# Attention block on one core: VectorE's share of the softmax exponentials as a sum of four 16-bit patterns

## The chip, the core and the metric

The kernel runs on one core of a Trainium2 chip. The metric is the device time of one launch in microseconds (us), lower is better. A core has five engines that run their own instruction streams and meet at semaphores: TensorE (PE, matmuls; its weight loads are shown as PEld), VectorE (DVE), ScalarE (ACT), GpSimd (POOL) and SyncE (SP, which issues the DMAs). Matmuls write to PSUM, eight banks of 512 fp32 columns on 128 partitions.

## What is computed

A transformer block on 2048 tokens of width 640: a layer norm, attention with 32 heads of 20 dimensions without a mask, a residual, a second layer norm, and a gated GELU network of width 1728 with a residual.

```python
def _A_ref(x, wqkv, wo):                      # x is layernorm(A_x)
    qkv = (x @ wqkv).reshape(B, S, 3, H, Dh).transpose(2, 0, 3, 1, 4)
    q, k, v = qkv[0], qkv[1], qkv[2]          # B=1, H=32, S=2048, Dh=20
    scores = jnp.einsum("bhqd,bhkd->bhqk", q, k) * (Dh ** -0.5)
    o = jnp.einsum("bhqk,bhkd->bhqd", _softmax(scores), v)
    return o.transpose(0, 2, 1, 3).reshape(B, S, D) @ wo
h  = A_x + _A_ref(_layernorm(A_x), A_wqkv, A_wo)
n  = _layernorm(h)
h2 = h + (gelu(n @ w_gate) * (n @ w_up)) @ w_down
```

The 32 x 2048 x 2048 scores are 134 million exponentials, on 128 partitions about a million columns.

## The kernel before

**Tiling.** Heads go in groups of four (`NG` = 8): head j of a group uses row strip j of the array for its scores (20 dimensions in 32 rows, `tile_position=(32*j, 0)`) and column strip j for its values (21 columns, the last one sums the exponentials), so that four small matmuls run side by side. Queries are cut in chunks of 512, 512, 256, 256, 256, 128 and 128 (`SIZES`, numbered 0 to 6). A *tile* is one PSUM bank of scores, 128 keys by 512 queries or the same number of columns from more key blocks. A *slot* is 64 tiles that accumulate in one output bank: one group of heads in chunks 0 and 1, two in chunks 2 to 4, four in chunks 5 and 6; 32 slots in all. A *quad* is the four tiles of the four heads of a group for the same keys.

**Units.** `units` cuts the tiles of a slot into score units of two or three banks (`PAT`): banks 0 to 2 and 3 to 4 in turn, or, in chunks 1 to 3, banks 0 to 2 and 3 to 5. For each unit, `unit()` issues the score matmuls (L873), one ACT exp over the unit's banks into a ring of bf16 buffers (`pts` with `PR` = 12 tiles and `pts2` with `PR2` = 6), and value matmuls for two quads at a time (`PV_QUADS`) into bank 6. When a slot is complete, `epilogue()` copies bank 6 out, transposes and normalises.

**VectorE's share.** Some tiles per slot (`D_PER_SLOT`: 8 in most, 2 in the first) get their exponential from VectorE, in `d_exp`: the scores are scaled to int16 with 512 steps per octave (L831), and for two tiles at a time six operations correct the mantissa with a quadratic and give the bit pattern of a bf16. In the units of two banks (chunks 0 and 4 to 6) such a tile gets a bank of its own out of the background banks `BG`; in the units of three (chunks 1 to 3) it takes the place of one of ACT's. Its value matmul is put behind the unit at least `D_LAG` = 8 units later.

**Background.** While a chunk's exps run, `post()` does the output projection, the second layer norm and the gated network of the chunk before, in matmuls at low priority (L631, L1061, L1118) with VectorE emptying their banks. After the last chunk this work is the tail of the kernel.

**The order.** The order on each engine comes from a list scheduler (`Sched`) that runs at build time with costs written into each `op`: it walks through planned time, takes the ready operation of best priority (`P_QK` 0 for scores, `P_PV` 1 for values, `P_BG` 3 for background), and holds back a PE operation that would run past the moment at which the next scores are due. The engines then execute that order as it stands, each waiting at its semaphores. The scheduler also keeps the array busy: behind a value operation it adds filler matmuls (`sc.pad`, zeros into bank 6) until a window of 3.4 us is filled to `PAD_MIN`, and in empty moments it issues a full-width one (`sc.warm`). The filler behind value operations hangs on the tag of the operation:

```python
if e == "pe" and self.pad is not None and o.tag and o.tag[0] == "O":
```

Of the kernel before, what the change touches and what calls it, by code (L numbers as in the profile page):

```python
# [7 lines left out]
ALU = mybir.AluOpType  # L8
AX = mybir.AxisListType
FP32 = mybir.dt.float32  # L10
BF16 = mybir.dt.bfloat16
I32 = mybir.dt.int32
F16 = mybir.dt.float16
# [30 lines left out]
class Sched:  # L44
# [46 lines left out]
    def schedule(self):  # L91
# [23 lines left out]
        while done < total:  # L115
# [4 lines left out]
            for e in ENGINES:  # L120
# [8 lines left out]
                while ready[e]:  # L129
# [3 lines left out]
                    if e == "pe" and due is not None and o.prio[0] > 0 and t < due < t + o.dur + (MODE_SWITCH[e] if mode[e] not in (None, o.mode) else 0):  # L133
                        skipped.append((p, i))
                        if len(skipped) >= 60:
                            break
                        continue
# [165 lines left out]
VW = 21  # L303
# [15 lines left out]
CA, CB, CC = -0.277383, 1.25604202, 1.0 - 11.0 / 128  # L319
PV_QUADS = 2  # L320
D_LAG = 8
PR, PR2 = 12, 6
ND = 4
D_PER_SLOT = (8,8,8,8,8,8,6)
D_SLOT0 = 2
D_FIRST, D_SPAN = 1, 16
# [6 lines left out]
def bass_sequential_preLN__mha_block__glu_gated_geglu__prompt_kernel(  # L333
# [12 lines left out]
    with ExitStack() as es:  # L346
# [48 lines left out]
        E_WORDS = 19200  # L395
# [39 lines left out]
        dv = [ka[:, 1024 * i:1024 * i + 1024].bitcast(I16) for i in range(ND - 2)]  # L435
        pts2 = carve(PR2 * 512)


        carve = carver(qt_all[:, 0, :, :].rearrange("p g s -> p (g s)"), NG * 512)
        dv += [carve(1024).bitcast(I16) for _ in range(2)]  # L440
        df1 = carve(1024)
        dw1 = carve(1024).bitcast(F16)
        dv0 = [ha_f[:, 1024 * i:1024 * i + 1024].bitcast(I16) for i in range(ND)]
        df0, dw0 = ha_f[:, 1024 * ND:1024 * ND + 1024], ha_f[:, 1024 * ND + 1024:1024 * ND + 2048].bitcast(F16)
# [336 lines left out]
        PAT = [((0, 1, 2), (3, 4, 5)) if c in (1,2,3) else ((0, 1, 2), (3, 4)) for c in range(len(CHUNKS))]  # L781
        units, ubank, dtile, ends = [], [], [], []
        i, in_slot = 0, {}
        while i < len(tiles):
            s_ = tiles[i][0]
            c = slots[s_][0]
            bs = PAT[c][len(units) % 2]
            k = in_slot.setdefault(s_, [0, 0])
            nd = D_PER_SLOT[c] if s_ else D_SLOT0
            units.append(tiles[i:i + len(bs)])  # L790
            ubank.append(bs[0])
            six = len(PAT[c][1]) == 3
            i += len(units[-1])
            want = min(nd, (k[0] - D_FIRST) * nd // D_SPAN + 1) if k[0] >= D_FIRST else 0
            if six and k[1] < want and len(units[-1]) == 3 and units[-1][2][0] == s_:
                dtile.append(units[-1].pop())
                k[1] += 1
            elif not six and k[1] < want and tiles[i][0] == s_:
                dtile.append(tiles[i])
                k[1] += 1  # L800
                i += 1
            else:
                dtile.append(None)
            k[0] += 1
            ends.append(i)
        assert all(k[1] % 2 == 0 for k in in_slot.values())
        d_tiles = set(x for x in dtile if x)
        x_unit = {}
        for u, tl in enumerate(units):
            for x in tl + [dtile[u]]:  # L810
                x_unit[x] = u
        pv_bank = {}
        pv_open = set()
        pv_wait = []
        last_qk = {c: [] for c in range(len(CHUNKS))}
        d_raw, d_done = [], []
        d_n = [0]
        d_ops = []
# [3 lines left out]
        def d_exp(b, tile, prio):  # L822

            i, h = (d_n[0] // 2) % ND, d_n[0] % 2
            d_n[0] += 1
            assert all(x[1] != ("dv", i) for x in d_done)
            early = slots[tile[0]][0] == 0
            v = (dv0 if early else dv)[i]
            df, dw = (df0, dw0) if early else (df1, dw1)
            aft = tuple(e_ops) if early else tuple(e_ops) + tuple(last_qk[0])  # L830
            d_ops.append(op("dve", lambda eng: eng.tensor_scalar(v[:, 512 * h:512 * h + 512], bank(b), EXP_MUL, -32000.0,  # L831
                                                                 ALU.mult, ALU.max), c_dve(512), P_QK,
                            reads=[("SD", tile)], writes=[("dv", i)], rel=[b], after=aft))
            d_raw.append(tile)
            if h == 0:
                return
            zi = df.bitcast(I16)
            d = lambda fn, n, r, w: d_ops.append(op("dve", fn, 0.066 + n, prio, reads=r, writes=w))
            d(I("tensor_scalar", zi, v, 511, 2048, ALU.bitwise_and, ALU.bitwise_or), 0.265, [("dv", i)], ["df"])
            d(I("tensor_scalar", dw, zi, CA / OCT, CB, ALU.mult, ALU.add), 0.265, ["df"], ["dw"])  # L840
            d(I("tensor_tensor", dw, dw, dw, ALU.mult), 0.53, ["dw"], ["dw"])
            d(I("tensor_tensor", dw, dw, zi, ALU.mult), 0.53, ["df", "dw"], ["dw"])
            d(I("tensor_tensor", v, v, dw, ALU.add), 0.53, ["dw", ("dv", i)], [("dv", i)])
            d(I("tensor_scalar", v, v, 0.25, 16256.0 + 128.0 * (CC - 1.0), ALU.mult, ALU.add), 0.265, [("dv", i)], [("dv", i)])
            for k, tl in enumerate(d_raw):
                d_done.append((v[:, 512 * k:512 * k + 512].bitcast(BF16), ("dv", i), tl))
            d_raw.clear()

        def unit(u):
# [56 lines left out]
            while pv_wait:  # L906

                quads = []
                while pv_wait and len(quads) < PV_QUADS:
                    x0 = pv_wait[0][2]  # L910
                    have = [x for x in pv_wait if x[2][:3] == x0[:3]]
                    want = 4 - sum(1 for j in range(4) if x0[:3] + (j,) in d_tiles)
                    if len(have) < want or quads and quads[0][0][2][0] != x0[0]:
                        break
                    del pv_wait[0:want]
                    quads.append(have)
                if not quads:
                    return
                s_ = quads[0][0][2][0]
                c, gs = slots[s_]  # L920
                q0, nq = CHUNKS[c]
                nk = 512 // nq
                final = quads[-1][0][2][1:3] == (gs[-1], NT // nk - 1)
                if len(quads) < PV_QUADS and not final:
                    pv_wait[0:0] = [x for h in quads for x in h]
                    return

                for have in quads:
                    for x in list(d_done):
                        if u - x_unit[x[2]] >= D_LAG and x[2][3] not in [y[2][3] for y in have]:  # L930
                            have.append(x)
                            d_done.remove(x)
                while final and d_done:
                    have = []
                    for x in list(d_done):
                        if x[2][3] not in [y[2][3] for y in have]:
                            have.append(x)
                            d_done.remove(x)
                    quads.append(have)
                if s_ not in pv_bank:  # L940
                    pv_bank[s_] = bk = Bank(6)
                    acq = [bk]
                else:
                    bk, acq = pv_bank[s_], []
                fns, reads = [], ["vones", "zer"] + k_keys[0][0]
                for have in quads:
                    for kk in range(nk):
                        for pt, pkey, (_, g, kb, j) in have:
                            kt = kb * nk + kk
                            o = 512 * 6 + nq * gs.index(g)  # L950
                            fns.append(I("matmul", PS[32 * j:32 * j + VW, o:o + nq], v_all[:, kt, 4 * g + j, :],
                                         pt[:, kk * nq:(kk + 1) * nq], start=(s_, j) not in pv_open, stop=(kt == NT - 1),
                                         tile_position=(0, 32 * j), skip_group_check=True))
                            pv_open.add((s_, j))
                            reads += [pkey, ("v", kt, g // 4)]
                pv = op("pe", fns, 0.218 * len(quads), P_PV, mode="col", util=0.213 * len(quads), reads=reads, writes=[("O", s_), "pvseq"], acq=acq)
                if final:
                    sc.final.add(pv)
                    assert not d_done and not d_raw
                    epilogue(s_, bk)  # L960

# [182 lines left out]
        for s_, (c, gs) in enumerate(slots):  # L1144
# [27 lines left out]
            while ui < len(units) and ends[ui] - len(units[ui]) < slot_end[s_]:  # L1172
                unit(ui)
                ui += 1
# [36 lines left out]
```

## Time and profile before

| What | us |
|---|---|
| time, median of 3 runs | 927.22 |
| lowest and highest run | 923.36, 928.9 |
| profiled execution, span | 923.6 |
| ACT busy | 887.4 (96%) |
| PE busy | 835.0 (90%) |
| VectorE busy | 760.3 (82%) |
| POOL busy | 34.4 (4%) |
| exps of ACT, all forms (busy) | 954.0 |
| fillers of zeros, L354 `ps<-kt_all,zer` (busy) | 51.9 |
| mean granted TensorE clock | 0.996 |

The span is that of one profiled execution, from the first to the last instruction; it stands at the lower end of the runs. Busy times of one group count each instruction from its start to its end, and instructions of an engine overlap at their ends (that is how the exps' 954.0 fit into 887.4), so the spacing of starts, not the mean duration, tells what one more of a kind costs. A line such as L354 is that of a helper which many operations go through; the names of what is written and read tell them apart.

### The profile page before, as it was taken

To read this page: it belongs to the slowest core of one execution; us is meant where nothing else is said; L and a number is where in the kernel's file an instruction comes from. 1 tells how busy PE (TensorE), PEld (TensorE's weight loads), DVE (VectorE), ACT (ScalarE), POOL (GpSimd) and SP (SyncE) were. 2 spreads that over 40 slices of the span, in tenths; PEclk is the share of its full clock that TensorE was granted. 3 is DMA by queue.
4 is the path that set the end of the run, shared out by engine and by line. 5 is a ranking of instruction groups with operands and counts; after the bars stand their busy time and mean duration, and the time that the engine had idled before them with its cause. 6 is when DMAs were issued, how large, how long until landed. Compare 5 with 4: busy or idle time off the path is not lost.

```text
span 923.6 us, 23026 instructions
## 1 busy us (share of the span) xinstructions
PE 835.0 (90%) x10070; PEld 353.3 (38%) x10070; DVE 760.3 (82%) x1562; ACT 887.4 (96%) x786; POOL 34.4 (4%) x117
## 2 busy tenths in 40 slices
PE   3999999999998997999788997889999999998998
PEld 2432232222222222233233332334445455565666
DVE  8859999899897896888698995878898769997653
ACT  7899999999999999999999999999999999999981
POOL 5000000000001000000001000000101000001000
PEclk9999999999999999999999999999999999999999
DMA  7301021222721000000111000000100000110000
GB/s 258 95 21 41 17 55 48 71 56 67 228 99 30 1 2 1 1 8 16 37 30 30 2 2 1 2 23 24 44 17 16 1 9 23 26 37 10 10 16 16
DMA packets 39516, 34.36 MB, mean 37 GB/s; under 512 B 19436, under 2 KB 36936, under 8 KB 39416
## 3 DMA queue, kind: packets, MB, share of 16 engines
q1 hardware_dynamic: 39416, 32.89, 12.6%
q8 instruction: 79, 1.29, 0.6%
q14 instruction: 21, 0.17, 0.1%
HBM read 20.12 MB, written 8.09 MB: 31 GB/s over the span
## 4 chain that ended last, share of the span: by engine, by line
ACT 73%; PE 20%; DVE 4%; DMA 2%; SPq 0%; issue 0%
ACT pts L354 46%; ACT rege L354 26%; PE ps L873 5%; PE ps L1061 5%; PE ps L354 4%; PE ps L631 3%; PE ps L1118 3%; DMA regw<-in_A_wqkv_dram 1%; DVE rege L354 1%; ACT L354 1%; DVE rege L831 1%; DVE qt_all L354 1%; PE ps L576 0%; DMA rege<-o_nat 0%; DVE rege L1107 0%; SPq L354 0%
## 5 line engine op out<-in xcount | busy, mean ns | idle before, releaser
L354 ACT ACTIVATE pts<-ps 128x1536 bf16<-128x1536 f32 (+1 forms) x474 | 573.2, 1378 | 5.6 <-PE ps L873 4.5
L873 PE MATMUL ps<-qt_all,kt_all 32*128 32x256 bf16 (+2 forms) x3584 | 289.6, 289 | 48.9 <-ACT pts L354 28.3
L354 ACT ACTIVATE rege<-ps 128x1536 bf16<-128x1536 f32 (+1 forms) x230 | 292.1, 1380 | 2.1 <-PE ps L873 1.1
L873 PEld LDWEIGHTS ps<-qt_all,kt_all 32*128 32x128 bf16 x3584 | 91.3, 92 | 271.5 <-ACT pts L354 155.9
L1061 PE MATMUL ps<-rege,regw 128*128 128x256 bf16 (+2 forms) x980 | 159.2, 292 | 10.5 <-DVE rege L1107 4.8
L354 DVE TENSOR_TENSOR qt_all<-qt_all 128x1024 f16<-128x1024 f16 (+1 forms) x235 | 160.6, 683 | 3.3
L831 DVE TENSOR_SCALAR rege<-ps 128x512 int16<-128x512 f32 x152 | 104.3, 686 | 39.7 <-PE ps L873 38.8
L354 PE MATMUL ps<-pts,v_all 128*21 128x256 bf16 (+2 forms) x2122 | 136.3, 290 | 0.0
L354 PE MATMUL ps<-rege,v_all 128*21 128x256 bf16 (+2 forms) x1278 | 108.2, 292 | 0.0
L1061 PEld LDWEIGHTS ps<-rege,regw 128*128 128x128 bf16 x980 | 73.3, 98 | 70.9 <-issue 24.1
L631 PE MATMUL ps<-regw 128*128 128x512 bf16 (+1 forms) x360 | 87.0, 350 | 2.9 <-DVE v_all L764 1.4
L1118 PE MATMUL ps<-regw,rege 128*128 128x320 bf16 x448 | 78.3, 301 | 2.6 <-DVE rege L1107 1.6
L354 DVE TENSOR_SCALAR qt_all<-qt_all 128x1024 int16<-128x1024 int16 (+1 forms) x188 | 75.9, 420 | 1.5
L831 DVE TENSOR_SCALAR qt_all<-ps 128x512 int16<-128x512 f32 x94 | 64.3, 684 | 3.3 <-PE ps L873 3.0
L354 DVE TENSOR_TENSOR rege<-rege 128x1024 f16<-128x1024 f16 (+4 forms) x103 | 65.4, 644 | 0.8
L354 PEld LDWEIGHTS ps<-pts,v_all 128*21 128x21 bf16 x2122 | 49.2, 91 | 38.2 <-issue 32.6
L354 DVE TENSOR_SCALAR rege<-rege 128x1024 int16<-128x1024 int16 (+2 forms) x136 | 55.4, 424 | 1.2
L354 PE MATMUL ps<-kt_all,zer 128*32 128x512 bf16 x608 | 51.9, 385 | 0.0
L1107 DVE TENSOR_TENSOR rege<-rege,ps 128x512 bf16<-128x512 bf16 (+1 forms) x53 | 35.8, 678 | 19.3 <-PE ps L1061 19.1
L1118 PEld LDWEIGHTS ps<-regw,rege 128*128 128x128 bf16 x448 | 36.9, 98 | 32.2 <-issue 12.4
L354 PEld LDWEIGHTS ps<-rege,v_all 128*21 128x21 bf16 x1278 | 39.2, 91 | 19.8 <-issue 14.5
L631 PEld LDWEIGHTS ps<-regw 128*128 128x128 bf16 x360 | 28.6, 98 | 47.1 <-issue 21.9
(95 smaller groups left out, 579.3 us busy)
## 6 DMA issues: line engine op xcount, KB each, us to landing
rege<-in_A_x_dram SPq DMA_DIRECT2D x6, 640.0 KB, 5.3
q_rows<-regw SPq DMA_DIRECT2D x20, 128.0 KB, 1.7
out_dram<-rege SPq DMA_DIRECT2D x16, 160.0 KB, 1.8
regw<-in_B_w_gate_dram SPq DMA_DIRECT2D x1, 2160.0 KB, 11.5
regw<-in_B_w_up_dram SPq DMA_DIRECT2D x1, 2160.0 KB, 16.5
regw<-in_B_w_down_dram SPq DMA_DIRECT2D x1, 2080.0 KB, 21.6
kt_all<-k_rows SPq DMA_DIRECT2D x12, 160.0 KB
qt_all<-q_rows SPq DMA_DIRECT2D x12, 160.0 KB
```

Of the source, the lines that this page charges most:

```text
L354: return lambda eng: getattr(eng, method)(*args, **kwargs)
L631: yield op("pe", lambda eng, l=l, r=r, k=k: eng.matmul(bank(bk, n), l, r, start=(k == 0), stop=(k == len(steps) - 1)), c_mm(n), prio, mode ...
L831: d_ops.append(op("dve", lambda eng: eng.tensor_scalar(v[:, 512 * h:512 * h + 512], bank(b), EXP_MUL, -32000.0, ALU.mult, ALU.max), c_dve( ...
L873: return lambda eng: eng.matmul(out()[:, kk * nq:(kk + 1) * nq], kt_all[32 * j:32 * j + 32, g, kt * 128:(kt + 1) * 128], qt_all[32 * j:32 ...
L1061: op("pe", lambda eng, a=a, f=f, fi=fi: eng.matmul(bank(bk)[:, fi * nq:(fi + 1) * nq], w[:, a, F0[f]:F0[f] + 128], hnT[:, a, 128 * tb:128 ...
L1107: hdone.append(op("dve", lambda eng, bu=bu, fv=fv, w=w: eng.tensor_tensor(fv, fv, bank(bu, w), ALU.mult), c_dve(w), p, reads=[ku] + hkeys( ...
L1118: op("pe", lambda eng, f=f, o=o, hf=hf, bk=bk: eng.matmul(bank(bk, 320), ha_f[:, o:o + 128], wd[:, f, hf * 320:(hf + 1) * 320], start=(f = ...
```

## The change

**Exponential.** VectorE now takes whole quads, `D_QUADS` = 3, 3, 3, 2, 2, 2, 1 per slot of the seven chunks and none in the first slot: 79 quads. The four tiles of a quad are scaled to int16 as before into one buffer of 2048 columns. Then, in place of the quadratic, four operations (`TERMS`) each shift the same int16 values by another offset and give a bf16 bit pattern of 2048 columns; the sum of the four patterns stands for the exponential, and the sum is formed by the value matmuls, which run once for each of the four and accumulate in bank 6. The terms go to two or three buffers in turn (`d_a`).

**Units.** `SIX` is empty, so all chunks use units of three and two banks, and every VectorE tile gets a background bank. A quad's four score tiles are spread over the units from the slot's start (`D_FIRST` = 0, `D_SPAN` = 18).

**Value matmuls.** A new function `pv_op` issues them. An operation is two of ACT's quads or one term of one of VectorE's. The operations of a slot are tied to the first and the last one only, not to one another (`pvseq` is gone), and all but the last have the tag `"Oq"`. `D_LAG` is gone.

**Buffers.** `PR2` goes from 6 to 4 tiles; `E_WORDS` from 19200 to 19712.

**Scheduler.** When a PE operation is held back for the next scores, the moment at which these are due is now an event.

```diff
                     if e == "pe" and due is not None and o.prio[0] > 0 and t < due < ...:
                         skipped.append((p, i))
+                        if due not in events:
+                            heapq.heappush(events, due)
...
-CA, CB, CC = -0.277383, 1.25604202, 1.0 - 11.0 / 128
+TERM_LOG = 1233.0 / 512
+TERMS = tuple(128.0 * (127.0 - TERM_LOG) + o / 4.0 + 0.125 for o in (0, 90, 211, 365))
+NTERM = len(TERMS)
 PV_QUADS = 2
-D_LAG = 8
-PR, PR2 = 12, 6
-ND = 4
-D_PER_SLOT = (8,8,8,8,8,8,6)
-D_SLOT0 = 2
-D_FIRST, D_SPAN = 1, 16
+PR, PR2 = 12, 4
+D_QUADS = (3, 3, 3, 2, 2, 2, 1)
+D_QUADS0 = 0
+SIX = ()
+D_FIRST, D_SPAN = 0, 18
...
-        PAT = [((0, 1, 2), (3, 4, 5)) if c in (1,2,3) else ((0, 1, 2), (3, 4)) for c in range(len(CHUNKS))]
+        PAT = [((0, 1, 2), (3, 4, 5)) if c in SIX else ((0, 1, 2), (3, 4)) for c in range(len(CHUNKS))]
...
-            if h == 0:
+            if h < 3:
                 return
-            zi = df.bitcast(I16)
-            d = lambda fn, n, r, w: d_ops.append(op("dve", fn, 0.066 + n, prio, reads=r, writes=w))
-            d(I("tensor_scalar", zi, v, 511, 2048, ALU.bitwise_and, ALU.bitwise_or), 0.265, ...)
-            d(I("tensor_scalar", dw, zi, CA / OCT, CB, ALU.mult, ALU.add), 0.265, ["df"], ["dw"])
-            d(I("tensor_tensor", dw, dw, dw, ALU.mult), 0.53, ["dw"], ["dw"])
-            d(I("tensor_tensor", dw, dw, zi, ALU.mult), 0.53, ["df", "dw"], ["dw"])
-            d(I("tensor_tensor", v, v, dw, ALU.add), 0.53, ["dw", ("dv", i)], [("dv", i)])
-            d(I("tensor_scalar", v, v, 0.25, 16256.0 + 128.0 * (CC - 1.0), ALU.mult, ALU.add), 0.265, ...)
+            d_n[e] += 1
+            for off in TERMS:
+                a, ak = d_a[e][d_t[e] % len(d_a[e])]
+                d_t[e] += 1
+                d_ops.append(op("dve", I("tensor_scalar", a, v, 0.25, off, ALU.mult, ALU.add), 0.686, prio,
+                                reads=[vk], writes=[ak], after=aft))
+                pv_op([[(a[:, 512 * k:512 * k + 512].bitcast(BF16), ak, x) for k, x in enumerate(d_raw)]], tile[0])
             d_raw.clear()
+
+        def pv_op(quads, s_):
+            if s_ != pv_slot[0]:
+                d_wait.append((quads, s_))
+                return
...
+            pv_n[0] += len(quads)
+            first = not pv_ops
+            last = pv_n[0] == len(gs) * NT // nk + (NTERM - 1) * len(d_kb[s_])
...
+            i = op("pe", fns, 0.218 * len(quads), P_PV, mode="col", util=0.213 * len(quads), reads=reads,
+                   writes=[("O", s_)] if last else [("Oq", s_, pv_n[0])], acq=pv_ops[0:1] if first else [],
+                   after=pv_ops[1:] if last else pv_ops[1:2])
...
-                    for x in list(d_done):
-                        if u - x_unit[x[2]] >= D_LAG and x[2][3] not in [y[2][3] for y in have]:
-                            have.append(x)
-                            d_done.remove(x)
...
-                pv = op("pe", fns, 0.218 * len(quads), P_PV, mode="col", util=0.213 * len(quads), reads=reads, writes=[("O", s_), "pvseq"], acq=acq)
```

## The prediction

> **What bounds the kernel now.** I read the page's busy shares and its chain first.
>
> ```profile
> PE 835.0 (90%) x10070; PEld 353.3 (38%) x10070; DVE 760.3 (82%) x1562; ACT 887.4 (96%) x786; POOL 34.4 (4%) x117
> ACT 73%; PE 20%; DVE 4%; DMA 2%; SPq 0%; issue 0%
> ```
>
> ScalarE (ACT) works 96% of the span and is 73% of the chain that ended last. DVE, which the change relieves, is 4% of that chain. Next the groups with their shapes kept apart: what ACT does, and how often it waited.
>
> ```profile
> L354 ACT ACTIVATE pts<-ps 128x1536 bf16<-128x1536 f32 x263 | 400.6, 1569 | 5.5 <-PE ps L873 4.5 <-PE ps L354 0.7
> L354 ACT ACTIVATE pts<-ps 128x1024 bf16<-128x1024 f32 x211 | 240.4, 1139 | 0.1
> L354 ACT ACTIVATE rege<-ps 128x1536 bf16<-128x1536 f32 x131 | 201.1, 1569 | 1.8 <-PE ps L873 1.1 <-PE ps L354 0.5
> L354 ACT ACTIVATE rege<-ps 128x1024 bf16<-128x1024 f32 x99 | 111.9, 1131 | 0.4 <-PE ps L354 0.4
> ```
>
> There are 394 exps of three tiles and 310 of two, and together they waited 7.8 us. Their busy times overlap at the ends, so I take the spacing from the chain in order of time:
>
> ```profile
> 371.36 2.69 ACT rege L354 x2
> 374.04 5.37 ACT pts L354 x4
> 379.42 2.26 ACT rege L354 x2
> ```
>
> Two three-tile exps in a row take 2.69, so 1.344 us each (5.37 for four agrees). A three and a two take 2.26, so a two is 0.917 us. All exps: 394 x 1.344 + 310 x 0.917 = 813.8 us. The last one ends at 891.3; what follows is a tail of 923.6 - 891.3 = 32.3 us.
>
> **The change, part by part.** *Fewer tiles for ACT.* Of 2048 score tiles VectorE took 246 (2048 less 394 x 3 + 310 x 2); now 79 quads, 316. The order of the changed program has 346 exps of three tiles and 347 of two: 346 x 1.344 + 347 x 0.917 = 783.2 us. Gelus and table loads (16) are as many as before. **-30.6 us**, all on the chain.
>
> *VectorE.* A pair of tiles cost two readings of PSUM (0.69 each), three 1024-wide tensor_tensor (0.68) and three tensor_scalar (0.42): 4.7 us, 123 times, 576 us. A quad now costs four readings and four terms of 2048 columns, and such a tensor_scalar stands in the trace:
>
> ```profile
> L354 DVE TENSOR_SCALAR rege<-rege 128x2048 int16<-128x2048 int16 x2 | 1.4, 694 | 0.1
> ```
>
> 4 x 0.69 + 4 x 0.69 = 5.5 us, 79 times, 436 us. VectorE loses 140 us that bounded nothing: 0.
>
> *TensorE.* PE adds up the four terms, so each quad's value matmuls run four times: 237 more groups of four side by side. Costs by starts in the timeline:
>
> ```profile
> 400.45 0.39 PE L873 MATMUL ps<-qt_all,kt_all 32*128 32x512 bf16 x3
> 400.77 0.39 PE L354 MATMUL ps<-pts,v_all 128*21 128x512 bf16 x3
> 400.99 0.39 PE L354 MATMUL ps<-pts,v_all 128*21 128x512 bf16 x4
> 401.31 0.58 PE L1118 MATMUL ps<-regw,rege 128*128 128x320 bf16 x3
> 401.83 0.39 PE L873 MATMUL ps<-qt_all,kt_all 32*128 32x512 bf16 x3
> ```
>
> Four value matmuls take 0.215 us (400.77 to 400.99); a score group to the next kind takes 0.32, so a change of kind costs about 0.105. 237 x 0.215 = +51 us; 64 more changes of kind in the order, +7. Against it all 608 fillers `ps<-kt_all,zer` disappear from the order (152 groups, -33) and 57 of 84 full-width ones (-12). The 198 more score matmuls that now stand alone cost between 0.01 us (a group of four took 0.33 to the next kind, one of three 0.32) and 0.32 (one alone, at 103.40): 2 to 63, taken low, since each is put where its row strip is free. About +15 us, beside ACT: in a slot of chunk 1 PE has 21 x 0.215 (scores) + 12 x 0.06 + 25 x 0.215 (values) + 48 x 0.105 + some 4.5 of other matmuls = 20 us, against 10.4 pairs x 2.26 = 23.5 us of exps. I cost it at nothing; without that cover it is 15 us.
>
> *The ring of exp results.* It shrinks from 18 tiles to 16 (PR2 6 to 4). By PE's order, an exp whose buffer is freed by a value matmul queued behind that exp's own scores occurs 3 times in the old program and 15 times in the new; three of these 15 are in the first slot, where the first value matmul moves from behind five units' scores to behind seven and has 18 projection matmuls (18 x 0.134 = 2.4 us) about it. The old three are the waits of ACT for PE at L354 above: 0.7 + 0.5 + 0.4, about 0.5 each. 12 x 0.5 + 2 = **+8 us**; between 0 and a whole unit each, 15 x 1.13 = 17. I stay near the row.
>
> *The clock.* Fillers are added at value matmuls tagged `"O"`; most are now tagged `"Oq"`, so none is. What thin stretches cost is in the windows of before:
>
> ```profile
> 560.00:570.00 10.00, 6.39 (x49) 1.96 (x47) 4.22 (x7) 9.97 (x9) 0.00 (x0) 0.92 0.00 0
> 570.00:580.00 10.00, 9.05 (x113) 3.05 (x111) 8.84 (x16) 9.52 (x9) 0.00 (x0) 0.91 0.01 2
> ```
>
> The granted clock was 0.5 for 3.41 us from 568.35 and ACT lost 0.5 us (9.52). In the 3.41 us before, the array was filled 34% (columns of each matmul, a quarter where four run side by side); ahead of the second drop, at 896.03, 41%; stretches at 44% kept the full clock. Counting the new order in steps of three units, some 14 us in a dozen places lie below 42%: about five such windows, one or two more where starts bunch. 6 x 0.5 = **+3 us**; 0 to 8 (ten at 0.8). The Trainium skill, "TensorE: Matmul & The Clock Gate", section "What's actually happening", has the clock halve after an idle window of about 3.4 us. By that rule this term would be 0, for no PE gap comes near 3.4 us; the trace does not agree, since the longest gap before the drop at 568 was 1.65 us, and I follow the trace.
>
> *The tail.* Background matmuls get less room and pile up. After the last score group the old order has 250 gate/up matmuls of 128 columns and 56 of L1118; the new one 274, 70 more of 256 columns and 112 of L1118.
>
> ```profile
> 908.27 7.99 PE L1061 MATMUL ps<-rege,regw 128*128 128x128 bf16 x140 [0.39 <-ACT rege L582]
> 916.78 3.98 PE L1118 MATMUL ps<-regw,rege 128*128 128x320 bf16 x28 [0.51 <-DVE rege L1086]
> ```
>
> 128 columns take 0.057 (7.99/140), 256 then 0.108, L1118 0.134 (3.75/28 without the latency of the last): 24 x 0.057 + 70 x 0.108 + 56 x 0.134 = 16.5 us more. Chunk 4's two gelus and two table loads now stand ahead of the last exp, and about 5 us of this runs under them. PE's idle time after the last exp (3.3 us) and the 2 us lost to the half clock at 896 take another 5. **+6 us**, between 0 and 16.5.
>
> *No cost.* No DMA or POOL instruction is added or lost (152 and 122 in both orders).
>
> **Sum** against the profiled span of 923.6 (nothing lies around it: the runs shown are 923.4 to 928.9): -30.6 + 8 + 3 + 6 = -13.6, so 910.0. The median of the runs, 927.2, is 3.6 above this span; I keep that offset: **913.6 us**. Ends: 893.0 with no give-back; 893.0 + 17 + 8 + 16.5 = 934.5 with all.
>
> **Rivals.** *Nearly the whole gain (0.26).* The ring and the clock cost nothing because PE's slack, 20 against 23.5, recovers each delay. For: ACT waited only 7.8 us in 704 exps. Against: the 3 tight places did wait. 893.0 + 6 + 3.6 = 903.
>
> *The gain is used up (0.16).* Ring at a unit each, clock at 8, tail at 10: 893.0 + 17 + 8 + 10 = 928; with the offset, about no change. For: in the last slots PE's sum (31.2) equals ACT's (30.8).
>
> *PE waits for VectorE (0.17), slower.* Before, a VectorE tile's value matmul came eight units later (D_LAG) and PE waited for it almost never. Now each of 316 term groups is queued as soon as planned, with two or three term buffers in turn: if VectorE is late, PE stops in order, the next scores queue behind it, and ACT waits for them. If one of a quad's four rounds is late by one PSUM reading (0.69), 79 x 0.69 = 54 us, and half of it passes PE's slack: +27, 941. It decides from 22 us, or 0.28 per quad. Against: 436 us of term work in 850 leaves VectorE free to be early.
>
> **How the numbers follow.** Forecast 0.41, the rivals 0.26, 0.16 and 0.17. About 1% (9 us) is what a measurement tells from no change. Faster: 0.26, 0.37 of the forecast's 0.41 and a little of the second, 0.64. Same: 0.04 and most of the second, 0.18. Slower: 0.18. The forecast's own range is 905 to 921. For 8 in 10 it is 898 to 934: it holds most of the nearly whole gain and all of the used-up case, and leaves out the slower rival.
>
> **What would show it.** Right: 346 and 347 exps at 1.34 and 0.92; ACT waiting for PE at the value line (L357) some 8 us; several half-clock windows of 3.4 us; a tail of about 38 us after the last exp. Wrong: ACT waiting for scores (L911) by over 20 us with PE waiting for VectorE's terms ahead of it, which is the slower rival; or a clock of 1 throughout and a tail of 32.

## The result, and the profile after

The changed kernel takes 914.82 us (median of 4 runs, 912.81 to 918.82); the kernel before took 926.12 in the same comparison (4 runs, 923.36 to 928.9). The ratio is 0.9889 with a 95% interval of 0.9856 to 0.9922: 11 us faster. The profiled execution has a span of 913.2 us, 10.4 less than the 923.6 of before.

The page's first rows, busy shares and chain, for the changed kernel:

```profile
PE 861.3 (94%) x10905; PEld 371.0 (41%) x10905; DVE 651.7 (71%) x1210; ACT 859.8 (94%) x775; POOL 33.2 (4%) x117
PE 46%; ACT 45%; DVE 5%; DMA 2%; issue 0%; SPq 0%; DVEq 0%
```

ACT's work fell by 28 us and PE's rose by 26. The chain shows what this does: ACT was 73% of it and is now 45%, PE rose from 20% to 46%. The kernel has gone from a bound of one engine to one of two that take turns. DVE lost 109 us of busy time and is still only 5% of the chain. The exps by form, and ACT's waits:

```profile
L357 ACT ACTIVATE pts<-ps 128x1024 bf16<-128x1024 f32 x347 | 375.8, 1083 | 7.4 <-PE ps L357 3.8 <-PE ps L911 3.4
L357 ACT ACTIVATE pts<-ps 128x1536 bf16<-128x1536 f32 x231 | 347.7, 1505 | 7.4 <-PE ps L911 5.4 <-PE ps L357 1.5
L357 ACT ACTIVATE rege<-ps 128x1536 bf16<-128x1536 f32 x115 | 173.2, 1506 | 1.6 <-PE ps L911 1.1
```

There are 346 exps of three tiles and 347 of two. Their idle time (7.4 + 7.4 + 1.6) is 16.4 us where it was 7.8, partly for scores (L911) and partly at the value matmuls that free a ring buffer (L357). The chain in order of time gives their spacing:

```profile
416.76 1.34 ACT rege L357
418.10 5.44 ACT pts L357 x5
423.54 1.34 ACT rege L357
```

From 416.76 on, `rege` (three tiles), five `pts` (three of two tiles, two of three) and again `rege`: 1.34 for a three, and 3 x 0.917 + 2 x 1.344 = 5.44 for the five. These are the durations that the prediction used.

With them, the change of the span can be taken apart. "Lost" is what the spacing of two exps' ends exceeds 1.344 or 0.917 by, summed over the trace and given to the line that ended the wait; it counts every small delay, also those too short for the groups' idle column.

| Part | before | after | difference |
|---|---|---|---|
| exps at their spacing | 813.8 | 783.2 | -30.6 |
| start of the first exp | 35.26 | 36.09 | +0.8 |
| lost while waiting for scores | 4.1 | 11.4 | +7.3 |
| lost at value matmuls (ring) | 2.0 | 6.2 | +4.3 |
| end of the last exp | 891.3 | 873.2 | -18.1 |
| from there to the end | 32.3 | 40.0 | +7.7 |
| span | 923.6 | 913.2 | -10.4 |

(The first four differences sum to -18.2; rounding leaves 0.1.) The 7.3 us of score waits have two parts. One is the half clock. In 10-us windows of the trace (the columns after the span of a window are the five engines' busy times, PEclk, DMA share and GB/s):

```profile
72.00:82.00 10.00, 9.42 (x72) 2.73 (x72) 8.63 (x18) 8.91 (x9) 0.00 (x0) 0.83 0.16 44
313.00:323.00 10.00, 9.10 (x61) 2.07 (x57) 7.14 (x13) 8.65 (x8) 0.62 (x1) 0.72 1.02 172
328.00:338.00 10.00, 9.64 (x81) 2.21 (x83) 6.65 (x11) 8.84 (x8) 0.00 (x0) 0.85 1.03 374
```

PEclk of 0.83, 0.72 and 0.85 where PE counts as more than 90% busy. The clock was 0.5 for 3.41 us from 75.00, for 6.83 from 317.35 and for 3.41 from 327.59: four windows of 3.41 us, in which score waits lost 3.6 us. The other part is a single wait. The timeline at 190 us:

```profile
189.85 1.90 PE L632 MATMUL ps<-regw 128*128 128x512 bf16 x8
191.68 0.30 PEld L911 LDWEIGHTS ps<-qt_all,kt_all 32*128 32x128 bf16 x6 [0.42 <-DMA qt_all<-bounds]
191.69 0.60 PE L911 MATMUL ps<-qt_all,kt_all 32*128 32x512 bf16 x6
192.12 1.02 ACT L357 ACTIVATE pts<-ps 128x1024 bf16<-128x1024 f32 x1 [3.40 <-PE ps L911]
```

In PE's order, 0.97 us of value matmuls (from 188.88) and eight projection matmuls (L632, 1.9 us) stand ahead of the first scores of a new group of heads, whose queries and keys arrive by DMA (`qt_all`). ACT waits 3.4 us for these scores.

### The profile page after: what moved, and what is told of

It reads as the page before. It is cut to its first block, busy times and chain, and to the rows that moved or that the text cites. A ratio compares the mean times of both kernels' runs of the same rounds, so it can differ in the third digit from the quotient of the medians.

```text
span 913.2 us, 24238 instructions
## 1 busy us (share of the span) xinstructions
PE 861.3 (94%) x10905; PEld 371.0 (41%) x10905; DVE 651.7 (71%) x1210; ACT 859.8 (94%) x775; POOL 33.2 (4%) x117
## 4 chain that ended last, share of the span: by engine, by line
PE 46%; ACT 45%; DVE 5%; DMA 2%; issue 0%; SPq 0%; DVEq 0%
ACT pts L357 34%; PE ps L911 13%; PE ps L357 11%; ACT rege L357 10%; PE ps L1053 7%; PE ps L632 7%; PE ps L1110 6%; DMA regw<-in_A_wqkv_dram 1%; DVE rege L832 1%; DVE rege L357 1%; DMA rege<-in_A_x_dram 1%; DVE qt_all L832 1%; ACT L357 1%; PE ps L976 1%; DVE qt_all L357 1%; PE ps L577 0%
## 5 line engine op out<-in xcount | busy, mean ns | idle before, releaser
L357 ACT ACTIVATE pts<-ps 128x1536 bf16<-128x1536 f32 x578 | 652.0, 1252 | 14.8 <-PE ps L911 8.8
L911 PE MATMUL ps<-qt_all,kt_all 32*128 32x256 bf16 (+2 forms) x3584 | 322.4, 290 | 20.2 <-ACT pts L357 11.2
L911 PEld LDWEIGHTS ps<-qt_all,kt_all 32*128 32x128 bf16 x3584 | 102.9, 92 | 236.9 <-ACT pts L357 130.2
L832 DVE TENSOR_SCALAR rege<-ps 128x512 int16<-128x512 f32 x200 | 137.4, 688 | 73.3 <-PE ps L911 71.2
L357 ACT ACTIVATE rege<-ps 128x1536 bf16<-128x1536 f32 x115 | 173.2, 1506 | 1.6 <-PE ps L911 1.1
L1053 PE MATMUL ps<-rege,regw 128*128 128x256 bf16 (+2 forms) x980 | 154.5, 290 | 3.8 <-DVE rege L1099 2.3
L357 PE MATMUL ps<-pts,v_all 128*21 128x256 bf16 (+2 forms) x2472 | 135.0, 288 | 0.0
L357 PE MATMUL ps<-rege,v_all 128*21 128x512 bf16 (+2 forms) x1564 | 127.9, 316 | 1.4 <-DVE rege L357 1.0
L1053 PEld LDWEIGHTS ps<-rege,regw 128*128 128x128 bf16 x980 | 74.3, 98 | 57.8 <-issue 26.1
L357 DVE TENSOR_SCALAR rege<-rege 128x2048 int16<-128x2048 int16 x132 | 88.8, 685 | 2.4 <-PE ps L357 1.1
L632 PE MATMUL ps<-regw 128*128 128x512 bf16 (+1 forms) x360 | 87.5, 352 | 2.0 <-DVE rege L832 0.9
L357 PEld LDWEIGHTS ps<-pts,v_all 128*21 128x21 bf16 x2472 | 54.3, 91 | 34.6 <-issue 28.3
L357 PEld LDWEIGHTS ps<-rege,v_all 128*21 128x21 bf16 x1564 | 41.3, 91 | 44.0 <-issue 24.4
L357 PE MATMUL ps<-qt_all,v_all 128*21 128x256 bf16 (+2 forms) x1048 | 53.7, 284 | 2.1 <-DVE qt_all L357 2.0
L632 PEld LDWEIGHTS ps<-regw 128*128 128x128 bf16 x360 | 29.2, 99 | 47.6 <-issue 26.3
L1088 DVE CAST rege<-ps 128x512 bf16<-128x512 f32 (+1 forms) x53 | 36.1, 680 | 16.2 <-PE ps L1053 16.0
L357 DVE TENSOR_SCALAR qt_all<-rege 128x2048 int16<-128x2048 int16 x70 | 47.0, 686 | 0.7
L357 DVE TENSOR_SCALAR qt_all<-qt_all 128x2048 int16<-128x2048 int16 x69 | 46.3, 685 | 1.7 <-PE ps L357 1.3
```

The costliest lines, as they stand in the source:

```text
L357: return lambda eng: getattr(eng, method)(*args, **kwargs)
L632: yield op("pe", lambda eng, l=l, r=r, k=k: eng.matmul(bank(bk, n), l, r, start=(k == 0), stop=(k == len(steps) - 1)), c_mm(n), prio, mode ...
L911: return lambda eng: eng.matmul(out()[:, kk * nq:(kk + 1) * nq], kt_all[32 * j:32 * j + 32, g, kt * 128:(kt + 1) * 128], qt_all[32 * j:32 ...
L1053: op("pe", lambda eng, a=a, f=f, fi=fi: eng.matmul(bank(bk)[:, fi * nq:(fi + 1) * nq], w[:, a, F0[f]:F0[f] + 128], hnT[:, a, 128 * tb:128 ...
L1088: cp.append(op("dve", lambda eng, bg=bg, fv=fv, w=w: eng.tensor_copy(fv, bank(bg, w)), c_dve(w), p, reads=[kg], writes=hkeys(k), rel=[bg], ...
```

## The experiments

Ratios are to the kernel before, run on the same chip.

### The ring alone

The old kernel, its ring of exp results cut from 18 tiles to 16.

```diff
-PR, PR2 = 12, 6
+PR, PR2 = 12, 4
```

> The kernel before with the ring of exp results at 16 tiles instead of 18 (PR2 6 to 4), nothing else. In its order 27 exps have the value matmul that frees their buffer queued behind their own scores, against 3. If such a place costs the half us read before (waits of ACT for PE's value line 1.6 us at 3 places), ACT's waits for the value line rise to 10 to 14 us and the time by about 12, to 938. The rival, that PE's slack absorbs a smaller ring, expects 926 to 929 and waits for the value line under 4 us.

930.79 us (929.5 to 930.85), ratio 1.0063 (1.0042 to 1.0084). The groups of its exps:

```profile
L354 ACT ACTIVATE pts<-ps 128x1536 bf16<-128x1536 f32 x280 | 420.9, 1554 | 7.1 <-PE ps L873 5.0 <-PE ps L354 1.3
L354 ACT ACTIVATE pts<-ps 128x1024 bf16<-128x1024 f32 x300 | 334.4, 1115 | 5.0 <-PE ps L354 4.7
```

The waits at the value line (L354) are now 4.7 us ahead of the two-tile exps, which hardly waited before. Lost at value matmuls: 8.3 us at 13 places, 2.0 at 3 before. So two tiles of ring cost about 6 us here, half of what the count of tight places had given (27 counted, 13 waited), and the time missed the expected 938 by 7 us: a counted place is worth some 0.3 us, not 0.5.

### The units alone

The old kernel with units of three and two banks in all chunks.

```diff
-        PAT = [... if c in (1,2,3) else ((0, 1, 2), (3, 4)) ...]
+        PAT = [... if c in () else ((0, 1, 2), (3, 4)) ...]
```

> The kernel before with units of three and two banks in all chunks, VectorE's quadratic and its 246 tiles as they were. ACT then has 360 exps of three tiles and 361 of two: 360 x 1.344 + 361 x 0.917 = 814.9 us against 813.8, so +1.1 us; 7 tight ring places against 3, +2. Expected 929, that is, units of 3 and 2 alone gain nothing. A rival is that the background gains from the second bank it gets in chunks 1 to 3: then the time falls below 923.

929.36 us (928.81 to 930.74), ratio 1.0047 (1.0028 to 1.0067). As expected: by themselves the units gain nothing; they lose 4 us. The background does gain, as the rival had it, but only what ACT pays for: the tail falls from 32.3 to 27.3 us, while the last exp ends 8.8 us later (one more gelu with its two table loads ahead of it, 4.3; more waits in the ring, 3.5; the exps themselves, 1.1). The gain is in the 70 tiles that ACT no longer has, not in their packing.

### No fillers in the old kernel

```diff
-                if e == "pe" and self.pad is not None and o.tag and o.tag[0] == "O":
+                if e == "pe" and self.pad is not None and False:
```

> The kernel before without the fillers behind value operations, nothing else. Counted in its order, about 23 us lie in stretches filled below 42%. The clock theory expects 6 to 9 windows of 3.41 us at half clock (against 1 before the tail) and 0.5 to 0.9 us for each, so 4 to 6 us more, about 930. The rival, that fillers only take PE time from the background, expects no more than two such windows before the tail and a time of 922 to 926.

936.66 us (929.42 to 937.46), ratio 1.0104 (1.0066 to 1.0141). The profiled execution, its fastest, has three stretches of half clock (13.65 us from 88.48, 6.83 from 163.57, 3.41 from 682.40: seven windows) and 10.1 us lost at scores instead of 4.1. In this kernel the fillers hold the clock; without them the time is longer, by 11 us where 5 had been expected, and spreads over 8 us.

### One term

The changed kernel with the value matmuls of the first of the four terms alone: VectorE's work and the exps stay, 237 groups of value matmuls go.

```diff
-                pv_op([[(a[:, 512 * k:...
+                if off == TERMS[0]: pv_op([[(a[:, 512 * k:...
-            last = pv_n[0] == len(gs) * NT // nk + (NTERM - 1) * len(d_kb[s_])
+            last = pv_n[0] == len(gs) * NT // nk + 0
```

> The changed kernel with the value matmuls of only the first of the four terms (the other three terms are still formed by VectorE and are left out of the sum). PE then has 237 groups of value matmuls fewer, 51 us. If these push the background into the tail, the tail after the last exp falls from 40 us to about 31 and the tight ring places outside the first slot vanish (-3 us); more thin stretches cost 3 to 5 us at the clock: about 903. If the term matmuls lie wholly beside ACT's work, tail and time stay at 40 and 913 to 916.

Its four runs took 944.43, 944.66, 925.49 and 941.48 us: less work, and slower, for even the fastest lies above every run of the changed kernel (918.82 at most). The first is profiled; its clock in 40 slices, and ACT's waits:

```profile
PEclk9997986999869879999999799999999999879999
ACT pts L357 <- PE ps L911: 36.6, 32, 10.2
ACT rege L357 <- PE ps L911: 9.7, 13, 1.2
```

The clock is below 0.9 in ten slices of the forty, 0.6 in two; in all it is halved for 122.9 us, 36 windows (not the 48 that an expectation below names); ACT waits 46 us for scores. PE has less to do, its array is filled less, and the clock halves; that the one leads to the other is borne out by the next experiment, where fillers bring the 122.9 us down to 23.9. A loss of this size was not foreseen. The expectation for the tail did hold: from the last exp to the end it is 28.9 us, against 40.0 with all four terms (27.6 and 28.0 in the two faster one-term kernels below). The longest wait, 10.2 us, is another matter, seen next.

### Fillers in the changed kernel, with and without the four terms

The tag of the new value operations is added to the condition, so that fillers are placed behind them.

```diff
-                if ... and o.tag and o.tag[0] == "O":
+                if ... and o.tag and o.tag[0] in ("O", "Oq"):
```

> The changed kernel with the fillers behind all its value operations again (the tag test accepts both tags; 456 zero matmuls, 114 groups, 24 us of PE). The clock theory expects at most two windows at half clock (4 in the changed kernel) and the 3.6 us that exps waited for scores in them gone. The tail theory expects the background pushed back by the fillers: the order has 51 us of PE work after the last score group against 42, so a tail some 9 us longer. Together 914 to 921. If fillers cost nothing, the time is about 911.

> As the run with the value matmuls of one term only (the other three terms are left out of the sum), and with the fillers back (596 zero matmuls, 149 groups, 32 us). If what that run lost was the clock alone, half-clock windows fall from 48 to at most 4, exps wait for scores under 10 us instead of 51, the tail stays at 29 us and the time is 897 to 904. If the wait for scores has another cause, it stays above 930.

With four terms 936.74 us (936.27 to 940.41), ratio 1.0136 (1.0106 to 1.0167): 22 slower than without fillers. With one term 922.11 (914.21 to 928.8), 0.9951 (0.992 to 0.9982). Both missed, by 16 and 18 us. In the profile of fillers with four terms the tail is 54.2 us (40.0): the fillers take the room of background matmuls, which move behind the last exp. Nor do they hold the clock here: it is halved for 23.9 us of the profiled execution, against 13.65 without them. And at 326 us something new stands, in three rows of the timeline, SP's queue, PE and ACT:

```profile
326.42 14.35 SPq L357 DMA_TRANSPOSE rege<-xn_t  x2
344.53 1.03 PE L1053 MATMUL ps<-rege,regw 128*128 128x512 bf16 x2 [7.97 <-DMA rege<-xn_t]
346.15 1.45 ACT L357 ACTIVATE pts<-ps 128x1536 bf16<-128x1536 f32 x1 [8.32 <-PE ps L911]
```

The DMA transposes of chunk 0's normalised rows (`xn_t`) hold the queue for 14.35 us. PE has a gate matmul (L1053) next that needs them; it waits 7.97 us, the scores queue behind it, and ACT waits 8.32. With one term and fillers it is a longer chain:

```profile
295.75 21.80 SPq L357 DMA_TRANSPOSE rege<-xn_t  x4
314.56 0.94 DVE L357 TENSOR_SCALAR xn_t<-rege,mu,rs 128x640 bf16<-128x640 bf16 x2 [13.01 <-DMA rege<-xn_t]
316.88 0.61 PE L357 MATMUL ps<-qt_all,v_all 128*21 128x512 bf16 x4 [11.87 <-DVE qt_all L357]
318.07 1.02 ACT L357 ACTIVATE pts<-ps 128x1024 bf16<-128x1024 f32 x1 [11.25 <-PE ps L911]
```

The first row merges four transposes: the first pair takes 15.5 us, then the queue waits 3.8 us for VectorE's next rows, and the second pair takes 2.5. VectorE waits 13.01 us to overwrite `xn_t` until the transposes have read it; behind that stand its readings and terms; PE waits 11.87 us for a term (`qt_all`), with the next scores behind; ACT waits 11.25. The last three rows are the mechanism of the slower rival, started by a DMA. What they meet is seen in a 10-us window of the first of the two variants, and in SP's queue. The window first:

```profile
330.00:340.00 10.00, 5.80 (x63) 1.71 (x63) 5.77 (x10) 7.83 (x8) 0.00 (x0) 0.92 1.04 385
```

The DMA engines are full (share 1.04) and move 385 GB/s. SP's queue of the changed kernel, and then of the kernel before:

```profile
308.92 2.63 SPq L357 DMA_TRANSPOSE rege<-xn_t  x2
313.15 2.52 SPq L357 DMA_TRANSPOSE rege<-xn_t  x2
317.50 0.45 SPq L357 DMA_DIRECT2D regw<-in_B_w_gate_dram  x1
```
```profile
239.27 0.45 SPq L354 DMA_DIRECT2D regw<-in_B_w_gate_dram  x1
287.83 5.75 SPq L354 DMA_TRANSPOSE rege<-xn_t  x4
```

The three weights of the gated network (2160 + 2160 + 2080 KB) are loaded when the projections have left `regw`. Before, this was 49 us ahead of the transposes. The changed kernel has 12 VectorE tiles instead of 8 per slot in chunk 0, so the projections there get less room and end later, and the loads are issued at 317.50, 78 us later. The queue has finished issuing the transposes 1.8 us earlier, at 2.6 us a pair; the second pair lands at 318.6, after 4.2 to 4.7 us instead of the first's 2.7, so it just touches the loads. In the variants the order is shifted a little, a pair meets the loads, and that pair takes 10.8 to 17.0 us (in the variant of this window the loads are issued at 322.44, the transposes at 326.42; the 10.2 us wait of the one-term kernel is of this kind, with 17.0). The changed kernel escapes this by less than 2 us.

The late loads do touch it in another way. From 302 to 332 us its trace has no matmul of the projections or of the network at all, since the first are done and the weights land between 328 and 340. Three of its four half-clock windows lie in this stretch, with 2.3 of the 3.6 us of score waits, and the fourth lies in the other such stretch of the first 100 us (70 to 82); others (246 to 260, 541 to 559) have no drop. The kernel before has stretches like it (231 to 255, 276 to 297), but with fillers, and keeps the clock there. No run moves the loads alone, so this is a reading of the traces and not a tested cause.

### Fewer quads late, and two in chunk 0

Two attempts at the tail and at the lateness: the first with fillers (up to 0.46), quads moved out of the last chunks and spread over 19 units; the second the changed kernel with two quads per slot in chunk 0.

```diff
-PAD_WIN, PAD_MIN = 3.4, 0.42
+PAD_WIN, PAD_MIN = 3.4, 0.46
-D_QUADS = (3, 3, 3, 2, 2, 2, 1)
+D_QUADS = (3, 3, 3, 2, 2, 1, 0)
-D_FIRST, D_SPAN = 0, 18
+D_FIRST, D_SPAN = 0, 19
```
```diff
-D_QUADS = (3, 3, 3, 2, 2, 2, 1)
+D_QUADS = (2, 3, 3, 2, 2, 2, 1)
```

> A candidate: the changed kernel with fillers behind all value operations (filled to 0.46), one quad per slot in chunk 5 and none in chunk 6 (75 quads instead of 79), and D_SPAN 19. ACT gets 16 tiles back, +7 us of exps; the order has 25 us of PE work after the last scores instead of 42, so the tail shrinks from 40 to about 32; half-clock windows 0 to 2, -3. Expected 907 to 913; if the tail does not depend on the last chunks' terms, 918 or more.

> The changed kernel with two quads per slot instead of three in chunk 0 (72 quads). ACT gets 28 tiles back: +12 us of exps. In its order the scores of head groups 6 and 7 are no longer queued behind 4.5 us of other work for their late K and Q rows: the one wait of 3.5 us for scores at 192 us is gone. The tail falls by about 5 (fewer term groups ahead of it). Expected 915 to 919. If that wait has to do with something else than VectorE's and PE's load in chunk 0, it stays, and the time is 920 or more.

The first took 922.53 us (921.11 to 923.0), ratio 0.9967 (0.9954 to 0.998). It missed its expectation by 10 us. Its tail is 28.8 us, as intended; but the first pair of transposes, at 300.80, met the loads and took 10.8 us, and 9.4 us of exp time went at 318 to 324. The second took 927.76 (923.73 to 937.81), ratio 1.003 (0.9999 to 1.006), 9 us above what was expected. Its loads are issued at 211.58, nothing collides, and the wait at 192 us is gone, which supports that the late projections are the cause of both. But it loses the clock for 27.31 us from 248.75, in a stretch without background matmuls (204 to 269 us) that begins where the projections now end; one of its windows:

```profile
250.00:260.00 10.00, 10.00 (x54) 2.53 (x53) 6.15 (x11) 7.22 (x7) 0.00 (x0) 0.50 0.01 2
```

54 matmuls fill the 10 us at half clock, and ACT is busy 7.22 of them.

### No collision: chunk 0's transposes on PE

The kernels with fillers and with chunk 0's second layer norm transposed by PE, as the tail does it, instead of by DMA. One with all terms, one with one term.

```diff
-                if tail:
+                if tail or c == 0:
...
-                               banks, p, "act", after=first)
+                               banks, p, "act" if tail else "dve", after=first)
```

> The run after_filler with one more edit: chunk 0's second layer norm is transposed by PE instead of by DMA. In after_filler two of these DMA transposes took 14.4 us because they met the loads of the network's weights, a gate matmul waited 8.0 us for them, scores stood behind it, and exps lost 8.4 + 1.1 us at one place and four half-clock windows' worth. If that is the cause, no exp waits more than 4 us and the time falls from 936.7 by 9 to 12, to 925 to 928; what is left over the changed kernel is the longer tail. If the wait has another cause, it stays at 935 or more.

> The run after_one_term_filler (value matmuls of one term only, the other three left out of the sum; fillers back) with chunk 0's second layer norm transposed by PE. The collision cost 11.4 + 1.6 us of waits there. Expected: exps wait under 13 us in all (25.7 before), tail 28 to 29, time 899 to 904 in most runs. This bounds what the 237 extra groups of value matmuls cost when clock and collision are out of the way: 10 to 14 us against the changed kernel. If 914 or more remains, they cost nothing.

With four terms 931.65 us (927.81 to 933.47), ratio 1.0072 (1.0053 to 1.0091); with one 905.0 (902.72 to 913.49), 0.9799 (0.9744 to 0.9854). Both came out above their expectations, by 4 and 1 us. Against the same kernels with DMA transposes that is 5 and 17 us less; the waits at 318 and 346 us are gone. So the collision is shown as a cause. Its price at full clock, by the lines of the last experiment, is 7 us in both (927.2 to 920.5, 904.9 to 898.0); the rest of the 17 is the clock. The last exps end at 875.8 and 873.4, nearly together; the tails are 54.0 and 28.0. With fillers, then, the three extra rounds of value matmuls cost nearly all of their price in the tail: 26 of the 28 us between the two spans. And the clock is still halved for 27.3 us of the kernel with four terms, so neither the missing fillers nor the collision alone made it drop.

### A version that takes what was learned

Fillers, PE transposes for chunk 0, and VectorE's quads moved from the last two chunks to chunk 3.

```diff
-D_QUADS = (3, 3, 3, 2, 2, 2, 1)
+D_QUADS = (3, 3, 3, 3, 2, 1, 0)
-D_FIRST, D_SPAN = 0, 18
+D_FIRST, D_SPAN = 0, 19
```

> A candidate: the changed kernel with fillers behind all value operations, chunk 0's second layer norm transposed by PE, quads per slot 3, 3, 3, 3, 2, 1, 0 (79 again, moved from the last chunks to chunk 3) and D_SPAN 19. The exps are as many tiles as in the changed kernel; the order has 33 us of PE work after the last scores instead of 42 and hardly a stretch below 42%. Expected: half-clock windows 0 to 1 (-3), tail about 33 (-7), one collision less to fear: 904 to 910. If the tail stays at 40 or waits for scores stay above 11 us, 914 or more.

912.28 us (912.18 to 912.62), ratio to the kernel before 0.9862 (0.9834 to 0.9891). The first rows of its page:

```profile
span 910.4 us, 24782 instructions
PE 872.6 (96%) x11177; PEld 376.5 (41%) x11177; DVE 651.4 (72%) x1214; ACT 862.3 (95%) x775; POOL 31.4 (3%) x117
PEclk9999999999999999999999999999999999999999
```

The clock stays full over the whole span, the tail is 34.5 us and the runs lie within 0.5 us. It is 2.5 us below the changed kernel's median, though the two intervals overlap. It missed its expectation by 2 us: PE is busy 96%, and 20.3 us of small waits are left ahead of the exps (13.2 for scores at 73 places, 7.1 in the ring).

### What the clock costs, from all runs together

Each run has a span and a mean granted clock. If c is the clock, (1 - c) x 2 x span is the time at half clock. A straight line through the runs of one kernel gives the loss per microsecond of half clock and the span at full clock:

| Kernel | clock of the runs | loss per us at half clock | span at full clock |
|---|---|---|---|
| before (25 runs) | 0.994 to 1.0 | 0.36 | 921.1 |
| before, no fillers (5) | 0.974 to 0.987 | 0.33 | 919.6 |
| changed (4) | 0.987 to 0.994 | 0.41 | 907.4 |
| changed, one term (4) | 0.929 to 0.958 | 0.36 | 896.2 |
| changed, chunk 0 two quads (10) | 0.965 to 0.985 | 0.35 | 912.5 |
| one term, fillers (10) | 0.969 to 0.989 | 0.39 | 904.9 |
| one term, fillers, PE transposes (4) | 0.979 to 0.996 | 0.36 | 898.0 |
| fillers, PE transposes (8) | 0.982 to 0.991 | 0.34 | 920.5 |
| fillers (4) | 0.98 to 0.987 | 0.30 | 927.2 |
| fillers, fewer quads late (10) | 0.993 to 0.996 | 0.37 | 916.5 |

Ten kernels give 0.30 to 0.41 (the other three have runs too close in clock for a line): a window of 3.41 us at half clock goes with 1.0 to 1.4 us, and the spread of a kernel's runs goes with the number of such windows. It need not all be the clock's doing, since a long wait can also empty the array and bring on a drop. The last column is an estimate, the farther from the runs the rougher: its standard error is 0.2 us for the kernel before, 1.5 for the changed one, 5 for the one-term kernel. By it the change is worth 13.7 us at full clock (921.1 to 907.4), and the three extra rounds of value matmuls cost 11.2 without fillers (907.4 - 896.2), give or take 5. The last version has its span of 910.4 at full clock, so by this column it beats the changed kernel through the clock: its edits cost 3.0 us (910.4 - 907.4, twice the error), less than the windows that they prevent.

## Why the prediction was right

The forecast was 913.6 us and the time is 914.82; the likeliest case was the one that came. By its steps:

**Exps.** 346 and 347 at 1.34 and 0.92 us, -30.6: exact. The last exp ends at 873.2, which by the sum of -30.6, +8 and +3 was to be 871.7.

**VectorE.** Its readings and terms now take 434 us (217 + 217 in the groups), as counted. The engine's busy share fell by 109 us only, since the many short operations of before overlapped at their ends. On the time it is worth nothing, as said.

**The ring.** +8 forecast, 4.3 measured. The mechanism is right, L357 being where ACT waits; the price per tight place was too high, by the run with the ring alone (0.3 us, not 0.5).

**The clock.** +3 forecast; the waits inside its four windows are 3.6 us, and by the fitted line some 4.9 us of the span (13.6 us at 0.36) against 2.5 before. The number is right by two errors that cancel, which is luck: the windows were fewer than the five to seven counted, and each costs more than 0.5 us (0.9 by the waits inside, over 1 by the fitted line). The bound of 42% was half right. Ahead of the drop at 896.03 the prediction read 41%; the matmuls that start in those 3.41 us come to 22% by their columns, and to some 28% if the four fp32 transposes among them are taken at the 0.109 us that they are apart elsewhere in this trace. Counted so in all 13 traces (an estimate: 512 columns at 0.215 us, a quarter for a matmul on one strip; windows of 3.41 us from 30 us on, of which the drops of a trace lie whole multiples apart), all 15 windows filled to less than 30% were followed by a drop, of some 110 filled to 30 to 41% only 23 were, and of over 3000 fuller ones none. So windows above 42% are safe, as the prediction took it, but most windows just below it are, too; the changed kernel's drops came after windows of 33 to 41%, while others of 38% kept its clock. The Trainium skill, "TensorE: Matmul & The Clock Gate", section "What's actually happening", names an idle window of about 3.4 us as the condition for the halved clock, and calls the window free-running and the number of slow matmuls variable from run to run. That the outcome varies agrees with the spreads above (a clock of 0.987 to 0.994 in the changed kernel); the first part does not: in the 3.41 us before the drops of the changed kernel the longest gap between matmuls was 0.55 us. One drop elsewhere does fit it: in the one-term kernel the array was empty for the whole 3.41 us before 335.89.

**The tail.** +6 forecast, +7.7 measured. The work that piled up is as counted. The gelus (`rege<-rege`) that the prediction saw come ahead of the last exp had stood ahead of it before, too, at 847 us; what changed is that they now stand right before it, behind the last scores, and cover 5.9 us of that work:

```profile
867.62 3.28 ACT L357 ACTIVATE rege<-rege 128x2048 bf16<-128x2048 bf16 x2
872.22 1.02 ACT L357 ACTIVATE pts<-ps 128x1024 bf16<-128x1024 f32 x1
898.65 7.25 PE L1053 MATMUL ps<-rege,regw 128*128 128x128 bf16 x127
906.42 3.98 PE L1110 MATMUL ps<-regw,rege 128*128 128x320 bf16 x28 [0.52 <-DVE rege L1078]
```

The last exp starts at 872.22, and 41 us of background matmuls follow, the last of them here.

**PE, costed at nothing.** This is the weak step. The prediction had 15 us of PE work hidden beside ACT, and a tail term beside it. The one-term kernels point to the two being one thing: 237 groups of value matmuls, 51 us by their count, cost some 11 us of span by the fitted lines, and the tail alone differs by as much (28.9 against 40.0). What PE can't do beside the exps it does after them.

**What was missed.** Two small items, +0.8 for the first exp and 3.5 for the scores at 192 us. They and the tail's excess of 1.7 are 6 us; the ring gave back 3.7. So the span came out at 913.2, not 910.0; the offset to the median was 1.6, not 3.6, which hid most of that. What the sum had not at all is the shift of the weight loads by 78 us. The collision cost the changed kernel next to nothing, because its transposes are issued 1.8 us ahead of them; but three of its four half-clock windows lie where PE has no background work until these weights land.

**The rivals.** Nearly the whole gain: no, the waits did come. The gain used up: no, the ring didn't reach its upper bound. PE waiting for VectorE: in the changed kernel PE's waits for terms (`qt_all`, `rege`) are few and short, 2.0 us and 1.0 in the groups of value matmuls (their weight loads wait longer, 24.4 us in 77 pieces of at most 0.8, while other matmuls still run), and the 11.4 us lost at scores are half of the 22 from which that rival decides. The chain that it described does occur, in one variant and for 11 us, when VectorE itself is held by a DMA.

**Open.** Which of the windows filled to between 30 and 41% lose the clock, and so why the number of drops differs from run to run. The ring at 18 tiles in the changed kernel was not tried.

## What to carry to other kernels

Work taken off the busiest engine is paid where its replacement lands: here 31 us of ScalarE became 51 us on TensorE, of which most hid or took the place of fillers and some 11 came out in the tail, so the tail belongs in the sum of every change that adds to an engine with background work. An order written at build time has collisions that no engine's busy share shows: look where large loads and short latency-critical DMAs come to stand when a stage is squeezed. And compare kernels at an equal granted clock, by a line through their runs, before a few microseconds are given to a cause.

## What the runs showed of the hardware

- The clock halves in a busy stretch when the array is thinly filled, and less work on PE can therefore be slower: with a quarter of the value matmuls for VectorE's tiles the four runs took 925.49 to 944.66 us at a clock of 0.929 to 0.958, where all four terms took 914.82 at 0.987 to 0.994. Ahead of the changed kernel's drops no gap between matmuls was over 0.55 us.
- By an estimate of the fill from the columns, all 15 windows of 3.41 us filled to less than 30% were followed by half clock, 23 of some 110 filled to 30 to 41%, and none of over 3000 fuller ones (13 traces).
- A microsecond of half clock goes with 0.30 to 0.41 us of span, in ten kernels.
- A pair of DMA transposes that takes 2.5 to 2.6 us alone takes 10.8 to 17.0 us beside 6.4 MB of weight loads (four kernels).
